# A row norm's small VectorE instructions moved to ScalarE, its guard to a 385th element of the row, and its overflow test to one place

## The chip, the core and the metric

The kernel runs on one core of a Trainium2 chip. A core has five engines with a queue of instructions each: TensorE (PE in the profile, PEld for its weight loads), VectorE (DVE), ScalarE (ACT), GpSimd (POOL) and SyncE (SP, which issues all DMAs here). Engines run side by side and wait for each other by semaphores; each works through its own queue in order. The metric is the device time of one execution in microseconds; lower is better.

## What is computed

A decaying linear attention over 4 sequences of 768 positions with 8 heads of 48, then two gated feed-forward layers on the 3072 rows of 384, the first behind a root-mean-square norm:

```python
for t in range(S):
    cur = np.einsum('bhd,bhe->bhde', u[None] * kt, vt)
    y[:, :, t] = np.einsum('bhd,bhde->bhe', rt, state + cur)
    state = w[None, :, :, None] * state + np.einsum('bhd,bhe->bhde', kt, vt)
...
rms = np.sqrt(np.mean(x * x, axis=-1, keepdims=True) + 1e-06)
xn = x / rms * rms_g
g = xn @ w_gate
x = (g / (1.0 + np.exp(-g)) * (xn @ w_val)) @ w_out
...
gate = 1.0 / (1.0 + np.exp(-(x @ w_gate2)))
out = (gate * (x @ w_val2)) @ w_out2
```

The weights are doubles (d_ff = 1536).

## The kernel before

**Tiles and stages.** The 3072 rows are 24 tiles of 128 (`attention(i)`, tile `i` is positions `128*(i // 4)` of sequence `i % 4`). Four tiles make a block of 512 rows; six blocks go through layer 1 and then six through layer 2. A step (`step`) is one block times one of the 12 slices of 128 of d_ff: 18 matmuls of 128x512 for gate and value (lines 687 to 689: high times high, high times low, low times high part of split fp32 operands) and 9 for the output (line 714). 144 steps stand behind each other on TensorE; the first needs all four tiles of block 0.

**One tile of attention.** `kq` and `rq` are k and r scaled by decay (line 474, on VectorE or GpSimd, whichever the planner finds free), turned by TensorE (line 332; ScalarE copies them out as `kT`, `rT`, line 498). Tiles 8 to 23 are turned by DMA through memory instead. `both` (lines 508 and 513) makes the products of 64 positions and the state's increments in two PSUM banks. VectorE masks the products (`aa`, line 519, one per bank), adds the state to the increments of the first bank (`zh`, line 529; for tiles 0 to 3, where there is no state yet, a plain copy, line 527) and then forms `zu` (line 532). `result` (lines 541, 548) makes the output, and VectorE adds the position's own term `vc` to it (line 554, two halves).

**The norm of a tile**, which is what the change is about: ScalarE squares the row and sums it (line 563; the sum is read out by a second, small instruction), VectorE tests the sum against 3e38 and keeps the verdict in `ok` (line 565), VectorE turns the sum into mean plus 1e-6 (line 568), GpSimd takes it to the power -0.5 (recorded under the helper's line 473), and VectorE scales the row (line 572). Then TensorE turns `x` (line 583) and ScalarE and VectorE write its high and low part `xh`, `xl` (lines 587, 589).

**The weights.** A piece is 128 rows of one of the three matrices as doubles. ScalarE (lines 66, 71), VectorE (lines 80, 81) and GpSimd (line 87) turn it into fp32, then ScalarE and VectorE split it (lines 649, 652). There are 36 pieces per layer; those of layer 1 are converted just ahead of the steps of block 0, those of layer 2 later.

**Order.** `Plan` collects tasks with an engine, a cost and a due time and runs them in a model of the engines; the order in which it starts them is the order of the instructions in the program, on every engine. So a task that costs less, goes to another engine or has other inputs can move all that stands behind it, SyncE's DMAs too. `V`, `A`, `G`, `T`, `S` are VectorE, ScalarE, GpSimd, TensorE and SyncE.

Of the kernel before, what the change touches and what calls it, by code (L numbers as in the profile page):

```python
# [7 lines left out]
F32 = mybir.dt.float32  # L8
# [3 lines left out]
AF = mybir.ActivationFunctionType  # L12
ALU = mybir.AluOpType
AX = mybir.AxisListType

P = 128
HS = 112
NPAIR = 4
EPS = 1e-6
# [211 lines left out]
def blocked(  # L231
# [17 lines left out]
    nc = tc.nc  # L249
    B, H, S, D = r.shape  # L250
    NT, DM = out.shape
# [11 lines left out]
    def ring(name, n, shape, dtype=F32):  # L263
        return [work.tile(shape, dtype, name=f"{name}{i}") for i in range(n)]
# [12 lines left out]
    ok = const.tile([P, 1], F32, name="ok")  # L277
    one = const.tile([P, 1], F32, name="one")
    totals = const.tile([P, 2 * 3 * NF], F32, name="totals")
    mhalf = const.tile([P, 1], F32, name="mhalf")  # L280

    rn, kn, vn = ring("rn", 2, [P, H, PAD]), ring("kn", 2, [P, H, PAD]), ring("vn", 3, [P, H, D])
    kq, rq, vc = ring("kq", 2, [P, H, PAD]), ring("rq", 1, [P, H, PAD]), ring("vc", 2, [P, H, D])
    cf, ss, small = ring("cf", 2, [P, H, 1]), ring("ss", 2, [P, 1]), ring("rms", 2, [P, 2])

    kT, rT, aa = ring("kT", 2, [HS, NPAIR, P]), ring("rT", 2, [P, NPAIR, P]), ring("aa", 1, [P, 2, NPAIR, P])
    x, z = ring("x", 2, [P, DM]), ring("z", B, [HS, NPAIR, D])

    zh, zu = ring("zh", 2, [HS, NPAIR, D]), ring("zu", 2, [HS, NPAIR, D])
    xh, xl = ring("xh", 2, [P, KC, N], F32R), ring("xl", 2, [P, KC, N], F32R)
# [26 lines left out]
    h = hi.bitcast(F32)  # L319

    def mul(e, out, x, y, op=ALU.mult):
        e.tensor_tensor(out=out, in0=x, in1=y, op=op)
# [11 lines left out]
    def setup():  # L334


        nc.vector.memset(o[0], 0.0)
        def warm(banks):
            for bank in banks:
                nc.tensor.matmul(state_of(plan.banks[bank]), o[0][:, :P], o[0][:, :NPAIR * D], start=True, stop=True)  # L340

        def turn_raw(bank, t):
            turn_pairs(plan.banks[bank], t)
            return pairs(plan.banks[bank])
        nc.vector.memset(wT, 1.0)
        for n in range(2):
            nc.sync.dma_start(out=wT[rows(n)], in_=w.rearrange("(p a) d -> a d p", a=2)[n])
        for t in (kn[0], rn[0], kq[1], rq[0]):
            nc.gpsimd.memset(t[:, :, D:], 0.0)
        load_heads(kn[0], k, 0, 0)  # L350
        load_heads(rn[0], r, 0, 0)
        nc.sync.dma_start(out=flat(u_bc), in_=u.rearrange("(o h) d -> o (h d)", o=1).to_broadcast([P, DM]))
        nc.sync.dma_start(out=g_bc, in_=rms_g.rearrange("(o c) -> o c", o=1).to_broadcast([P, DM]))
        nc.gpsimd.memset(mhalf, -0.5)
        nc.scalar.activation(one, mhalf, AF.Silu)
        nc.gpsimd.memset(ident, 0.0)
        nc.gpsimd.affine_select(out=ident, in_=ident, compare_op=ALU.not_equal, fill=1.0,
                                base=0, pattern=[[-1, P]], channel_multiplier=1)
# [12 lines left out]
        tp, tq = (t[:HS].rearrange("p (q t) -> p q t", q=NPAIR) for t in o[1:3])
        def lost(a, b):

            mul(nc.vector, sq[:, a:b], h[:, a - 1:b - 1], h[:, a - 1:b - 1])
            mul(nc.vector, low[:, a:b], sq[:, a:b], h[:, a:b], ALU.subtract)
            mul(nc.vector, twice[:, a:b], sq[:, a:b], h[:, a:b], ALU.add)

        def longer(e, s):
            n = 1 << s
            bc = p2[:, s].unsqueeze(2).to_broadcast([HS, NPAIR, n])  # L380
            if e is nc.vector:
                mul(e, tq[:, :, half - 2 * n:half - n], tq[:, :, half - n:half], bc)
# [12 lines left out]
        nc.vector.tensor_copy(p2[:, 0], wsafe)
        nc.vector.memset(tq[:, :, half - 1:half], 1.0)
        nc.gpsimd.memset(tp[:, :, half:half + 1], 1.0)
        mul(nc.vector, lo[:, 0], wsafe, h[:, 0], ALU.subtract)
        mul(nc.vector, both[:, 0], wsafe, h[:, 0], ALU.add)
        longer(nc.gpsimd, 0)  # L400
        lost(1, LOST)
        for i in range(1, 7):
            if i == LOST - 1:
                lost(LOST, 8)
            if i > 1:
                longer(nc.vector, i - 2)
            twofold(i)
            if i < 6:
                longer(nc.gpsimd, i)
        longer(nc.vector, 5)  # L410
        nc.vector.reciprocal(out=p2[:, 0], in_=p2[:, 6])
        bc = p2[:, 0].unsqueeze(2).to_broadcast([HS, NPAIR, half])
        mul(nc.vector, tq[:, :, half:], tq[:, :, :half], bc)
        mul(nc.gpsimd, tp[:, :, :half], tp[:, :, half:], bc)
        mul(nc.vector, kT[0], raw_k, tq)
        mul(nc.vector, rT[0][:HS], raw_r, tp)
        for i, (src, dst) in enumerate(((tq, wk), (tp, wr))):
            ps = plan.banks[i]
            for p in range(NPAIR):
                nc.tensor.transpose(ps[:, p * P:p * P + HS], src[:, p, :], ident[:HS, :HS])  # L420
            nc.scalar.activation(heads(dst), heads(ps.rearrange("p (h d) -> p h d", h=H)), AF.Copy)
# [43 lines left out]
    def attention(i):  # L465
# [58 lines left out]

        u3 = lambda sp: state_of(sp)[:HS].rearrange("p (q e) -> p q e", q=NPAIR)
        if first:
            add("V", 0.27, d + 4, lambda sp: nc.vector.tensor_copy(zh[i2], u3(sp)), [name("sp")], [("zh", i2)], psum=banks[:1])
        else:
            add("V", 0.27, d + 4, lambda sp: nc.vector.tensor_tensor(out=zh[i2], in0=u3(sp), in1=z[b], op=ALU.add),
                [name("sp"), ("z", b)], [("zh", i2)], psum=banks[:1])  # L530
# [27 lines left out]
        if not last:  # L558
            add("VG", (0.27, 0.6), d + 10, either(z[b], zu[i2], wc, ALU.mult), ["wc", ("zu", i2)], [("z", b)])


        t = ss[i2]
        add("A", 0.5, d + 7, lambda: nc.scalar.activation(flat(vc[i2]), x[i2], AF.Square, accum_out=t[:, 0:1]),
            [("x", i2)], [("vc", i2), ("ss", i2)])
        add("V", 0.07, d + 20, lambda: nc.vector.scalar_tensor_tensor(
            out=ok, in0=t[:, 0:1], scalar=3e38, in1=ok, op0=ALU.is_le, op1=ALU.mult), [("ss", i2)], ["ok"])
        t_ = small[i2]
        add("V", 0.07, d + 8, lambda: nc.vector.tensor_scalar(
            out=t_[:, 0:1], in0=t[:, 0:1], scalar1=1.0 / DM, scalar2=EPS, op0=ALU.mult, op1=ALU.add),
            [("ss", i2)], [("rms", i2)])  # L570
# [196 lines left out]
    def weights_ok():  # L767
        nc.vector.tensor_scalar(out=totals, in0=totals, scalar1=W_TOP * 2.0 ** -64, scalar2=None, op0=ALU.is_le)
        nc.vector.tensor_reduce(out=one, in_=totals, axis=AX.X, op=ALU.min)
        mul(nc.vector, ok, ok, one)  # L770
        nc.vector.tensor_scalar(out=ok, in0=ok, scalar1=-1.0, scalar2=1.0, op0=ALU.mult, op1=ALU.add)
        nc.vector.memset(one, 1.0)

# [7 lines left out]
    for n, (bi, f) in enumerate(steps):  # L781
# [9 lines left out]
                park_weights(*pieces[m], 3 * n + 6, begun)  # L791
            parks += PARK
        if (bi, f) == (turn - 1, NF - 1):
            plan.add("V", 0.6, at[turn, 3], weights_ok, [("total", i) for i in range(2 * 3 * NF)], ["ok"])
            plan.add("T", 0.1, at[turn, 3], count_bad, ["ok"], ["count"], psum=["count"])
            plan.add("V", 0.1, at[turn, 3], lambda ps: nc.vector.tensor_copy(bad, ps[:1, 0:1]), ["count"], psum=["count"])
        if bi == turn - 1:
# [168 lines left out]
```

## Time and profile before

| | |
|---|---|
| runs | 1031.54, 1032.00, 1032.87 us; median 1032.0 |
| profiled execution | 1029.34 us, its span 1027.7 us |
| busy: TensorE, its weight loads, VectorE, ScalarE, GpSimd | 98%, 81%, 48%, 33%, 14% of the span |
| mean granted clock of TensorE | 0.989 of full speed |
| chain that ended last | TensorE 87%, VectorE 8%, DMA 1%, ScalarE 1%, no wait shown 1% |

A busy share is the time in which at least one instruction of the engine was under way. Matmuls overlap and their ends are modelled, so TensorE is best read by its waits and by the starts of its instructions. The chain is followed back from the last instruction to whatever released each step.

### The profile page before, as it was taken

The page shows a single profiled execution, that of the slowest core. Times are in us where ns is not written, and L with a number is a line of the kernel's source. Part 1 is how long each engine was busy: PE and PEld are TensorE (multiplying, and loading weights), DVE is VectorE, ACT ScalarE, POOL GpSimd, SP SyncE. Part 2 cuts the span into 40 slices and gives each one's busy share as a digit, 9 for nine tenths or more (in the row PEclk, how much of TensorE's full clock was granted, in tenths as well). Part 3 has the DMA queues.
Part 4 walks back from the last instruction along what each step waited for, and adds up shares of the span by engine and source line. Part 5 has one row for each costly group of instructions (what it writes and reads, how often), then busy time and mean ns, then how long its engine had stood idle before and what let it go on. Part 6 is the DMA issues. An engine that isn't in the chain of part 4 may idle for free.

```text
span 1027.7 us, 19397 instructions
## 1 busy us (share of the span) xinstructions
PE 1002.4 (98%) x7938; PEld 831.1 (81%) x7938; DVE 490.4 (48%) x993; ACT 341.7 (33%) x710; POOL 140.2 (14%) x170
## 2 busy tenths in 40 slices
PE   7799999999999999999999999999999999999997
PEld 6577777787787777778888888888888888888886
DVE  7889995645655664653555322222222223222222
ACT  3577552223333333334555312222212222112221
POOL 4443432212321320211110000000000000000000
PEclk8899999999999999999999999999999999999998
DMA  8916356555884785653654100100100000000001
GB/s 195 274 41 157 91 110 143 106 104 129 178 175 123 156 189 135 145 148 94 198 171 147 62 1 3 59 1 22 40 1 31 32 1 5 27 1 27 4 1 34
DMA packets 213761, 91.40 MB, mean 89 GB/s; under 512 B 156576, under 2 KB 205984, under 8 KB 213664
## 3 DMA queue, kind: packets, MB, share of 16 engines
q1 hardware_dynamic: 213664, 90.08, 35.3%
q8 instruction: 64, 1.05, 0.5%
q14 instruction: 33, 0.27, 0.1%
HBM read 64.10 MB, written 25.95 MB: 88 GB/s over the span
## 4 chain that ended last, share of the span: by engine, by line
PE 87%; DVE 8%; DMA 1%; ACT 1%; issue 1%; POOL 0%; SPq 0%; DVEq 0%; POOLq 0%; ACTq 0%
PE bank L714 27%; PE bank L687 18%; PE bank L688 18%; PE bank L689 18%; PE bank L548 2%; DVE wraw L81 1%; PE bank L541 1%; PE bank L508 1%; DVE w L652 1%; DVE wt L80 1%; DVE hl L699 1%; DMA rn<-in_r_dram 1%; PE bank L513 1%; DVE vc L474 1%; DVE sg L696 0%
## 5 line engine op out<-in xcount | busy, mean ns | idle before, releaser
L687 PE MATMUL bank<-xh,w 128*128 128x512 f32 x864 | 344.5, 399 | 1.8 <-ACT w L649 1.1
L689 PE MATMUL bank<-xh,w 128*128 128x512 f32 x864 | 342.5, 396 | 0.3 <-DVE w L652 0.3
L688 PE MATMUL bank<-xl,w 128*128 128x512 f32 x864 | 342.6, 397 | 0.0
L696 DVE TENSOR_TENSOR sg<-bank,sg 128x512 f32<-128x512 f32 x144 | 99.2, 689 | 371.5 <-PE bank L689 368.2
L689 PEld LDWEIGHTS bank<-xh,w 128*128 128x128 f32 x864 | 162.7, 188 | 40.7 <-DVE w L652 2.3
L687 PEld LDWEIGHTS bank<-xh,w 128*128 128x128 f32 x864 | 162.8, 188 | 39.2 <-ACT w L649 2.4
L688 PEld LDWEIGHTS bank<-xl,w 128*128 128x128 f32 x864 | 162.8, 188 | 35.4 <-DVE xl L589 0.3
L694 ACT ACTIVATE sg<-bank 128x512 f32<-128x512 f32 x144 | 85.9, 597 | 294.0 <-PE bank L689 293.9
L698 ACT ACTIVATE hh<-sg 128x512 fp32r<-128x512 f32 x144 | 90.7, 630 | 238.5 <-DVE sg L696 238.5
L714 PE MATMUL bank<-w,hh 128*128 128x384 f32 x576 | 158.7, 337 | 0.0
L714 PE MATMUL bank<-hh,w 128*128 128x512 f32 x432 | 151.3, 401 | 0.7 <-DVE w L652 0.7
L699 DVE TENSOR_TENSOR hl<-sg,hh 128x512 fp32r<-128x512 f32 x144 | 102.2, 710 | 65.3 <-ACT hh L698 65.0
L714 PEld LDWEIGHTS bank<-w,hh 128*128 128x128 f32 x576 | 105.0, 188 | 3.4
L714 PEld LDWEIGHTS bank<-hh,w 128*128 128x128 f32 x432 | 81.0, 188 | 21.2 <-DVE w L652 1.6
L714 PE MATMUL bank<-w,hl 128*128 128x384 f32 x288 | 96.7, 336 | 0.0
L714 PE MATMUL bank<-hl,w 128*128 128x512 f32 x216 | 85.4, 395 | 0.0
L87 POOL TENSOR_TENSOR wt<-wraw 128x384 int32<-128x384 int32 x36 | 33.1, 918 | 200.1 <-DVE wraw L81 118.8
L66 ACT ACTIVATE wt<-wraw 128x384 f32<-128x384 f32 x72 | 39.7, 552 | 51.5 <-DMA wraw<-in_moe_w_gate_dram 23.0
L714 PEld LDWEIGHTS bank<-w,hl 128*128 128x128 f32 x288 | 54.1, 188 | 3.3 <-DVE hl L699 0.3
L714 PEld LDWEIGHTS bank<-hl,w 128*128 128x128 f32 x216 | 40.6, 188 | 8.7
L87 POOL TENSOR_TENSOR wraw<-wraw 128x384 int32<-128x384 int32 x36 | 37.8, 1060 | 54.4 <-DVE wraw L81 31.4
L81 DVE SCALAR_TENSOR_TENSOR wraw<-wraw,wt 128x384 int32<-128x384 int32 x72 | 41.8, 589 | 1.4
(122 smaller groups left out, 712.6 us busy)
## 6 DMA issues: line engine op xcount, KB each, us to landing
wraw<-in_moe_w_gate_dram SPq DMA_DIRECT2D x24, 384.0 KB, 4.4
wraw<-in_moe_w_val_dram SPq DMA_DIRECT2D x24, 384.0 KB, 4.5
wraw<-in_moe_w_out_dram SPq DMA_DIRECT2D x24, 384.0 KB, 5.0
parked<-wt SPq DMA_DIRECT2D x36, 192.0 KB, 2.7
wt<-parked SPq DMA_DIRECT2D x36, 192.0 KB, 2.4
kn<-in_k_dram SPq DMA_DIRECT2D x24, 192.0 KB, 3.7
rn<-in_r_dram SPq DMA_DIRECT2D x24, 192.0 KB, 4.1
vn<-in_v_dram SPq DMA_DIRECT2D x24, 192.0 KB, 3.8
```

The costliest lines, as they stand in the source:

```text
L66: nc.scalar.activation(t.bitcast(F32), raw[:, :, 1].bitcast(F32), AF.Abs, scale=2.0 ** -112, accum_out=total)
L81: yield nc.vector.scalar_tensor_tensor(out=high, in0=high, scalar=-(1 << 31), in1=t, op0=ALU.bitwise_and, op1=ALU.bitwise_or)
L87: nc.gpsimd.tensor_tensor(out=out, in0=raw[:, :, 1], in1=raw[:, :, 0], op=ALU.add)
L548: nc.tensor.matmul(yp[n][part(s)][ts, p * D:(p + 1) * D], aa[0][part(s), n, p, ts], vn[i3][part(s), 2 * p + n, :], start=(first and not s ...
L687: nc.tensor.matmul(ps, whi[f][:, kind, ws], xh[b2][:, c, :], start=(c == 0), stop=False)
L688: nc.tensor.matmul(ps, whi[f][:, kind, ws], xl[b2][:, c, :], start=False, stop=False)
L689: nc.tensor.matmul(ps, wlo[f][:, kind, ws], xh[b2][:, c, :], start=False, stop=(c == KC - 1))
L694: add("A", 0.6, d - STEP, lambda g: nc.scalar.activation(sg[n2], g, gate), [("g", n)], [("sg", n2)], psum=[("g", n)])
L696: add("V", 0.69, d + 1 - STEP, lambda ps: nc.vector.tensor_tensor(out=sg[n2], in0=ps, in1=sg[n2], op=ALU.mult), [("value", n)], [("sg", n2 ...
L698: add("A", 0.63, d + 1 - STEP, lambda: nc.scalar.activation(hh[n2], sg[n2], AF.Copy), [("sg", n2)], [("hh", n2)])
L699: add("VG", (0.69, 1.5), d + 1 - STEP, lambda e: by[e].tensor_tensor(out=hl[n2], in0=sg[n2], in1=hh[n2].bitcast(F32), op=ALU.subtract), [( ...
L714: nc.tensor.matmul(a[:, :rhs.shape[-1]], lhsT, rhs, start=(f == 0 and i == 0), stop=(f == NF - 1 and i == 2))
```

## The change

Three things. The copy of the state's increments for tiles 0 to 3 goes from VectorE to ScalarE. The tiles `x` and `vc` get a 385th column; that of `x` is set once by GpSimd, and ScalarE squares 385 elements of the row scaled by the root of 1/384, so that its sum is already the mean plus the guard; GpSimd's power reads that sum directly, and line 568 is gone. The sums of all 24 tiles are kept in `squares` and tested at once, with three VectorE instructions in `weights_ok`, in place of line 565 in every tile.

```diff
+    squares = const.tile([P, NTILE], F32, name="squares")
...
-    cf, ss, small = ring("cf", 2, [P, H, 1]), ring("ss", 2, [P, 1]), ring("rms", 2, [P, 2])
+    cf, small = ring("cf", 2, [P, H, 1]), ring("rms", 2, [P, 1])
...
-    x, z = ring("x", 2, [P, DM]), ring("z", B, [HS, NPAIR, D])
+    x_, vc_ = ring("x", 2, [P, DM + 1]), ring("vc", 2, [P, DM + 1])
+    x, vc = [t[:, :DM] for t in x_], [t[:, :DM].rearrange("p (h d) -> p h d", h=H) for t in vc_]
...
+        for t in x_:
+            nc.gpsimd.memset(t[:, DM:], (EPS * DM) ** 0.5)
...
         if first:
-            add("V", 0.27, d + 4, lambda sp: nc.vector.tensor_copy(zh[i2], u3(sp)), [name("sp")], [("zh", i2)], psum=banks[:1])
+            add("A", 0.27, d + 4, lambda sp: nc.scalar.activation(zh[i2], u3(sp), AF.Copy), [name("sp")], [("zh", i2)], psum=banks[:1])
...
-        t = ss[i2]
-        add("A", 0.5, d + 7, lambda: nc.scalar.activation(flat(vc[i2]), x[i2], AF.Square, accum_out=t[:, 0:1]),
-            [("x", i2)], [("vc", i2), ("ss", i2)])
-        add("V", 0.07, d + 20, lambda: nc.vector.scalar_tensor_tensor(
-            out=ok, in0=t[:, 0:1], scalar=3e38, in1=ok, op0=ALU.is_le, op1=ALU.mult), [("ss", i2)], ["ok"])
-        t_ = small[i2]
-        add("V", 0.07, d + 8, lambda: nc.vector.tensor_scalar(
-            out=t_[:, 0:1], in0=t[:, 0:1], scalar1=1.0 / DM, scalar2=EPS, op0=ALU.mult, op1=ALU.add),
-            [("ss", i2)], [("rms", i2)])
-        add("G", 0.55, d + 8, tt(nc.gpsimd, t_[:, 1:2], t_[:, 0:1], mhalf, ALU.pow), (), [("rms", i2)])
+        mean, t_ = squares[:, i:i + 1], small[i2]
+        add("A", 0.5, d + 7, lambda: nc.scalar.activation(vc_[i2], x_[i2], AF.Square, scale=DM ** -0.5, accum_out=mean),
+            [("x", i2)], [("vc", i2), ("square", i)])
+        add("G", 0.55, d + 8, tt(nc.gpsimd, t_, mean, mhalf, ALU.pow), [("square", i)], [("rms", i2)])
...
+        nc.vector.tensor_scalar(out=squares, in0=squares, scalar1=3e38 / DM, scalar2=None, op0=ALU.is_le)
+        nc.vector.tensor_reduce(out=one, in_=squares, axis=AX.X, op=ALU.min)
+        mul(nc.vector, ok, ok, one)
```

Line numbers of the changed kernel are a few higher: 474 becomes 480, 519 becomes 525, 554 becomes 560, 541 and 548 become 547 and 554.

**What moves.** VectorE, the last instructions ahead of the first step, whose matmuls need the fourth `xl` (tile 3; `x1` and `rms1` are tile 3's there, `x0` tile 2's, `bank3`, `bank1` with `aa0`, `zh0`, `zu0` are tile 4's, `w0` the first slice's weights). Before:

```order
L572 SCALAR_TENSOR_TENSOR x0_118<-x0_118,rms0_111,g_bc_85 128x384
L568 TENSOR_SCALAR rms1_112<-ss1_110 128x1
L565 SCALAR_TENSOR_TENSOR ok_91<-ss1_110,ok_91 128x1
L519 TENSOR_TENSOR aa0_117<-bank3_76,mask_87 128x4x64
L519 TENSOR_TENSOR aa0_117<-bank1_74,mask_87 128x4x64
L529 TENSOR_TENSOR zh0_124<-bank3_76,z0_120 112x192
L532 TENSOR_TENSOR zu0_126<-bank1_74,zh0_124 112x192
L589 TENSOR_TENSOR xl0_130<-bank6_79,xh0_128 128x3x128
L572 SCALAR_TENSOR_TENSOR x1_119<-x1_119,rms1_112,g_bc_85 128x384
L652 TENSOR_TENSOR w0_803<-wraw0_313,w0_803 128x384 x2
L589 TENSOR_TENSOR xl0_130<-bank2_75,xh0_128 128x3x128
```

Now:

```order
L80 TENSOR_SCALAR wt1_144<-wt1_144 128x384
L81 SCALAR_TENSOR_TENSOR wraw0_314<-wraw0_314,wt0_143 128x384
L589 TENSOR_TENSOR xl0_129<-bank2_75,xh0_127 128x3x128
L81 SCALAR_TENSOR_TENSOR wraw0_314<-wraw0_314,wt1_144 128x384
L572 SCALAR_TENSOR_TENSOR x1_116<-x1_116,rms1_109,g_bc_85 128x384
L80 TENSOR_SCALAR wt3_146<-wt3_146 128x384
L81 SCALAR_TENSOR_TENSOR wraw0_318<-wraw0_318,wt3_146 128x384
L589 TENSOR_TENSOR xl0_129<-bank3_76,xh0_127 128x3x128
L652 TENSOR_TENSOR w0_776<-wraw0_314,w0_776 128x384
```

Tile 4's masks and state stood ahead of the fourth `xl` and are now some 60 places behind it, among the steps; the split of the first weights moved behind it too. From the first mask of tile 1 on, 61 VectorE instructions stood up to and with the fourth `xl`; now there are 45.

TensorE at the same place (`vn1` with `aa0` and `z0` is tile 4's `result`, its `both` stands ahead of it; `x0` and `x1` are tiles 2 and 3). Before:

```order
L513 MATMUL bank1_74<-vn1_100,kq0_102 48x48
L583 MATMUL bank6_79<-ident_86,x0_118 128x128 x3
L541 MATMUL bank5_78<-z0_120,rT0_115 64x48
L548 MATMUL bank4_77<-vn1_100,aa0_117 32x48 x4
L583 MATMUL bank2_75<-ident_86,x1_119 128x128 x3
L687 MATMUL bank0_73<-xh0_128,w0_803 128x512
```

Now (`vn0` is tile 3's):

```order
L554 MATMUL bank7_80<-vn0_100,aa0_114 32x48 x4
L336 MATMUL bank6_79<-ident_86,kq0_103 112x128 x4
L583 MATMUL bank2_75<-ident_86,x0_115 128x128 x3
L583 MATMUL bank3_76<-ident_86,x1_116 128x128 x3
L687 MATMUL bank4_77<-xh0_127,w0_776 128x512
```

The first step stood behind all of tile 4's attention and now stands behind tile 3's; the turn of tile 4's `rq`, its `both` and its `result` come in steps 3 to 5.

VectorE at tile 1, with the engine whose semaphore each waits for. Before:

```order
L519 TENSOR_TENSOR aa0_117<-bank6_79,mask_87 128x4x64 [waits PE_49]
L519 TENSOR_TENSOR aa0_117<-bank7_80,mask_87 128x4x64 [waits PE_49]
L527 COPY zh1_125<-bank6_79 112x192
L568 TENSOR_SCALAR rms0_111<-ss0_109 128x1 [waits Activation_49]
L474 TENSOR_TENSOR vc1_106<-vn1_100,cf1_108 128x384 [waits DMAHW1_49]
```

Now:

```order
L525 TENSOR_TENSOR aa0_114<-bank6_79,mask_87 128x4x64 [waits Activation_49]
L480 TENSOR_TENSOR rq0_105<-rn0_96,wr_89 128x8x48 [waits DMAHW7_49]
L480 TENSOR_TENSOR vc1_118<-vn1_101,cf1_107 128x384 [waits DMAHW1_49,DVE_49]
L525 TENSOR_TENSOR aa0_114<-bank7_80,mask_87 128x4x64 [waits PE_49]
```

The first mask of each of tiles 0 to 3 waits for ScalarE's copy out of the same bank, and VectorE no longer stands at line 568 for ScalarE's sum.

## Rows read from the trace of the kernel before

**Rows 1.** Stretches of the span: us, busy us (instructions) of each engine, clock, DMA share.

```profile
core 0: us, PE busy (x) PEld busy (x) DVE busy (x) ACT busy (x) POOL busy (x), PEclk, DMA share, GB/s
0.00:46.10 46.10, 33.01 (x820) 27.94 (x820) 36.70 (x129) 19.27 (x51) 19.47 (x39) 0.85 0.93 223
46.10:150.00 103.90, 99.38 (x867) 76.22 (x868) 99.22 (x196) 68.82 (x170) 44.30 (x44) 0.98 0.44 110
150.00:360.00 210.00, 209.99 (x2529) 167.25 (x2528) 125.23 (x274) 62.10 (x132) 46.23 (x52) 1.00 0.65 139
...
470.00:1028.00 558.00, 550.15 (x2580) 472.03 (x2578) 166.79 (x265) 153.66 (x273) 9.87 (x11) 0.99 0.13 42
```

**Rows 2.** TensorE's timeline around the first step: start, us, line, [idle <- releaser].

```profile
41.38 0.26 PE L541 MATMUL bank<-zh,rT 48*64 48x48 f32 x2 [0.84 <-DVE zh L529]
...
46.11 0.79 PE L687 MATMUL bank<-xh,w 128*128 128x512 f32 x1 [0.58 <-ACT xh L587]
```

**Rows 3.** What TensorE waited for in 46:160: us in total, times, longest.

```profile
PE bank L687 <- ACT w L649: 1.1, 2, 0.8
PE bank L508 <- DVE xl L589: 0.8, 1, 0.8
...
PE bank L583 <- DVE x L572: 0.6, 1, 0.6
```

**Rows 4.** Two stretches of VectorE's load, columns as in rows 1.

```profile
20.55:46.09 25.54, 17.48 (x564) 14.09 (x564) 22.28 (x61) 11.24 (x29) 11.36 (x13) 0.87 1.00 262
46.11:138.30 92.19, 88.27 (x819) 67.51 (x819) 87.55 (x177) 63.76 (x160) 39.53 (x40) 0.98 0.44 113
```

**Rows 5.** VectorE's groups in 20.5:46: xcount | busy us, mean ns | idle before.

```profile
L519 DVE TENSOR_TENSOR aa<-bank,mask 128x256 f32<-128x256 f32 x8 | 3.1, 413 | 0.0
L565 DVE SCALAR_TENSOR_TENSOR ok<-ss,ok 128x1 f32<-128x1 f32 x4 | 1.7, 424 | 0.0
L527 DVE COPY zh<-bank 112x192 f32<-112x192 f32 x3 | 1.0, 347 | 0.0
L652 DVE TENSOR_TENSOR w<-wraw,w 128x384 fp32r<-128x384 f32 x2 | 1.0, 551 | 0.0
L568 DVE TENSOR_SCALAR rms<-ss 128x1 f32<-128x1 f32 x4 | 0.6, 146 | 0.0
```

**Rows 6.** The chain that ended last, in order of time: start, us, what.

```profile
14.01 6.85 DMA rn<-in_r_dram
...
148.21 2.10 PE bank L714 x9
```

**Rows 7.** TensorE's groups in 150:250.

```profile
L687 PE MATMUL bank<-xh,w 128*128 128x512 f32 x81 | 32.6, 403 | 0.0
L714 PE MATMUL bank<-hh,w 128*128 128x512 f32 x79 | 27.7, 402 | 0.0
L714 PE MATMUL bank<-hl,w 128*128 128x512 f32 x40 | 15.8, 395 | 0.0
L508 PE MATMUL bank<-rT,kT 48*64 48x64 f32 x192 | 4.2, 224 | 0.0
```

**Rows 8.** VectorE's groups in 46.6:140.

```profile
L565 DVE SCALAR_TENSOR_TENSOR ok<-ss,ok 128x1 f32<-128x1 f32 x4 | 2.3, 563 | 0.0
L474 DVE TENSOR_TENSOR vc<-vn,cf 128x384 f32<-128x384 f32 x3 | 2.3, 756 | 0.0
L474 DVE TENSOR_TENSOR kq<-kn,wk 128x384 f32<-128x384 f32 x4 | 2.2, 546 | 0.0
L568 DVE TENSOR_SCALAR rms<-ss 128x1 f32<-128x1 f32 x4 | 0.6, 144 | 0.0
```

**Rows 9.** ScalarE's groups over the whole span, shapes apart.

```profile
L498 ACT ACTIVATE rT<-bank 112x512 f32<-112x512 f32 x7 | 4.2, 595 | 4.8 <-PE bank L332 4.8
L421 ACT ACTIVATE wk<-bank 128x384 f32<-128x384 f32 x1 | 0.5, 491 | 4.6 <-PE bank L420 4.6
```

More of the change, by code (lines that the diff above doesn't have):

```diff
@@ L279, in blocked @@
     totals = const.tile([P, 2 * 3 * NF], F32, name="totals")
+    squares = const.tile([P, NTILE], F32, name="squares")
     mhalf = const.tile([P, 1], F32, name="mhalf")
     rn, kn, vn = ring("rn", 2, [P, H, PAD]), ring("kn", 2, [P, H, PAD]), ring("vn", 3, [P, H, D])
-    kq, rq, vc = ring("kq", 2, [P, H, PAD]), ring("rq", 1, [P, H, PAD]), ring("vc", 2, [P, H, D])
-    cf, ss, small = ring("cf", 2, [P, H, 1]), ring("ss", 2, [P, 1]), ring("rms", 2, [P, 2])
+    kq, rq = ring("kq", 2, [P, H, PAD]), ring("rq", 1, [P, H, PAD])
+    cf, small = ring("cf", 2, [P, H, 1]), ring("rms", 2, [P, 1])
     kT, rT, aa = ring("kT", 2, [HS, NPAIR, P]), ring("rT", 2, [P, NPAIR, P]), ring("aa", 1, [P, 2, NPAIR, P])
-    x, z = ring("x", 2, [P, DM]), ring("z", B, [HS, NPAIR, D])
+    x_, vc_ = ring("x", 2, [P, DM + 1]), ring("vc", 2, [P, DM + 1])
+    x, vc = [t[:, :DM] for t in x_], [t[:, :DM].rearrange("p (h d) -> p h d", h=H) for t in vc_]
+    z = ring("z", B, [HS, NPAIR, D])
     zh, zu = ring("zh", 2, [HS, NPAIR, D]), ring("zu", 2, [HS, NPAIR, D])
@@ L559, in attention @@
             add("VG", (0.27, 0.6), d + 10, either(z[b], zu[i2], wc, ALU.mult), ["wc", ("zu", i2)], [("z", b)])
-        t = ss[i2]
-        add("A", 0.5, d + 7, lambda: nc.scalar.activation(flat(vc[i2]), x[i2], AF.Square, accum_out=t[:, 0:1]),
-            [("x", i2)], [("vc", i2), ("ss", i2)])
-        add("V", 0.07, d + 20, lambda: nc.vector.scalar_tensor_tensor(
-            out=ok, in0=t[:, 0:1], scalar=3e38, in1=ok, op0=ALU.is_le, op1=ALU.mult), [("ss", i2)], ["ok"])
-        t_ = small[i2]
-        add("V", 0.07, d + 8, lambda: nc.vector.tensor_scalar(
-            out=t_[:, 0:1], in0=t[:, 0:1], scalar1=1.0 / DM, scalar2=EPS, op0=ALU.mult, op1=ALU.add),
-            [("ss", i2)], [("rms", i2)])
-        add("G", 0.55, d + 8, tt(nc.gpsimd, t_[:, 1:2], t_[:, 0:1], mhalf, ALU.pow), (), [("rms", i2)])
+        mean, t_ = squares[:, i:i + 1], small[i2]
+        add("A", 0.5, d + 7, lambda: nc.scalar.activation(vc_[i2], x_[i2], AF.Square, scale=DM ** -0.5, accum_out=mean),
+            [("x", i2)], [("vc", i2), ("square", i)])
+        add("G", 0.55, d + 8, tt(nc.gpsimd, t_, mean, mhalf, ALU.pow), [("square", i)], [("rms", i2)])
         add("V", 0.53, d + 9, lambda: nc.vector.scalar_tensor_tensor(
-            out=x[i2], in0=x[i2], scalar=t_[:, 1:2], in1=g_bc, op0=ALU.mult, op1=ALU.mult), [("rms", i2)], [("x", i2)], port=True)
+            out=x[i2], in0=x[i2], scalar=t_, in1=g_bc, op0=ALU.mult, op1=ALU.mult), [("rms", i2)], [("x", i2)], port=True)
         to = (slice(None), slice(None), slice(col * P, (col + 1) * P))
@@ L793, in blocked @@
         if (bi, f) == (turn - 1, NF - 1):
-            plan.add("V", 0.6, at[turn, 3], weights_ok, [("total", i) for i in range(2 * 3 * NF)], ["ok"])
+            plan.add("V", 0.6, at[turn, 3], weights_ok, [("total", i) for i in range(2 * 3 * NF)] + [("square", i) for i in range(NTILE)], ["ok"])
             plan.add("T", 0.1, at[turn, 3], count_bad, ["ok"], ["count"], psum=["count"])
```

## The prediction

> **What bounds the kernel now.** I read the busy shares first, then the load by stretches, since a share of 98% for TensorE says nothing of where the other 2% are. From 150 us on TensorE is busy without a gap, up to a single short wait and the kernel's tail, while VectorE has 40% of its time free and later 70% [rows 1]. Nothing that the change takes from VectorE there can move the end. Ahead of 150 us it is otherwise: up to 46 us TensorE is idle for 13 of 46 us, and from 46 to 150 VectorE is busy for 95% and TensorE loses 4.5 us [rows 1]. So the kernel has three parts: a start that ends with the first step, at 46.11 us [rows 2]; a stretch in which VectorE (weights, attention and the steps' own work) nearly sets the pace; and a long rest that belongs to TensorE. The time is, in effect, the start of the first step, plus all of TensorE's work behind it, plus what it waits in the second part.
>
> Both early parts show this norm. The last links ahead of the first step are ScalarE's `xh` and, before that, a `result` that waited for VectorE's `zh` [rows 2]; that `result` is tile 4's, which block 0 does not need, but it stands ahead of the first step in TensorE's queue. In the second part TensorE waits for split weights, for `xl`, and once for a row scaled by line 572 [rows 3].
>
> **The change, part by part.**
>
> *What the instructions cost.* Line 568 takes 0.15 us. Line 565 takes as little when VectorE is alone, but its mean is 0.42 us in the start and 0.56 us in the second part [rows 5, 8], where GpSimd works beside it. Up to 140 us the trace has eight of each: 1.7 + 2.3 us for line 565, 0.6 + 0.6 us for line 568. Four copies `zh` of 0.35 us are 1.4 us more [rows 5], where three of the four are. Together VectorE loses 6.6 us of work ahead of 140 us. That is the most that the bare removal could give if VectorE were the whole path there, and nothing is the least. The sixteen norms behind 140 us have TensorE's unbroken work as their cover; if that went, 16 x 0.3 us would be at stake. The three instructions of the common test run once, some 550 us in, under the same cover.
>
> *What is added.* ScalarE's four copies are bounded by what they replace, 0.35 us, and by a copy of 128x384 out of PSUM, 0.49 us [rows 9]; I take 0.4, near the lower, since the tile is half as wide. ScalarE is busy for 11 of the 25 us around them [rows 4], so its time is free. The 385th element and the two settings by GpSimd I cost at nothing: GpSimd is idle for over half of the start [rows 1]. The copy brings a wait, though: the mask of the same bank now waits for ScalarE, and all of VectorE's queue behind it. One copy (0.4) and two masks (0.33 each from start to start, by their mean of 0.41 less the overlap) are 1.06 us from `both` to the last of the three, against 0.33 + 0.33 + 0.35 = 1.01 us before: even. The trace of before has no bank that two engines read without a dependency of their own, so no row shows whether such a wait is needed. The Trainium skill's page "PSUM — Partial Sum Buffer" (PSUM bank collisions raise a hardware error) says that two engines must not touch one bank at the same time and that software has to keep them apart; by that rule the wait stays, and an overlap that would save some 0.3 us on each of four tiles is not to be had.
>
> *What moves: the start.* This is the largest term. The planner now puts tile 4's masks, `zh`, `zu`, `both` and `result` behind the first step. From 20.55 us to the fourth `xl` VectorE took 25.54 us, of which 22.28 were busy, in 61 instructions [rows 4]. In the new order 17 of them are no longer there. I subtract them at their means [rows 5]: line 565 1.7, line 568 0.6, three copies 1.0, three masks 1.2 (two of tile 4; the first of tile 1 comes ahead of my starting point), tile 4's `zh` and `zu` 0.7 (as the copy, 0.35 each), two splits of weights 1.0, one shift of weights 0.45; and add two products and one merge of weights that come in, at 0.55 each for a product of 128x384 [rows 8], and 0.4 more since the exchange of products with GpSimd is uneven. 22.3 - 6.65 + 2.05 = 17.7 us; the `rq` that now begins the list waits for its r, which landed at 20.86 us [rows 6]. Without any idle time the fourth `xl` would so come at 38.6 us, with the 3.3 us of idle time of before at 41.9. The other engines allow it: TensorE was busy for 17.5 of the 25.5 us with tile 4's work in them, ScalarE and GpSimd for 11 [rows 4]. I take 40.2, the middle, and the first step with it: 46.1 - 40.2 = 5.9 us earlier, between 7.5 and 4.2.
>
> *What moves: TensorE's work.* Tile 4 has not gone, it is behind the first step now. In 150:250 TensorE ran 3 x 81 matmuls of lines 687 to 689 (688 and 689 have as many as 687) and 119 of line 714, and six tiles of attention (192 records of line 508, 32 for each) [rows 7]. At 2.10 us for nine [rows 6], 0.233 us each, the 362 take 84.5 us, which leaves 15.5 us, or 2.6 for a tile. With the turn of `rq`, half a microsecond, 3.1 us go back.
>
> *What moves: VectorE's stretch.* Up to the last x of block 1, at 138.3 us, VectorE is busy for 87.6 of 92.2 us and TensorE idle for 3.9 [rows 4]. There VectorE loses 2.3 + 0.6 us [rows 8]. It gains tile 4's two masks (0.8), `zh` and `zu` (0.7), one split (0.55) and, counted in the new order, four more products (0.55 to 0.76 each [rows 8], 2.6): 4.7 us. Net 1.8 us more, while TensorE's own work there grows by 3.1. Where VectorE sets the pace, TensorE's idle time would shrink by 1.3 us; where single late weights do, it stays. I take 0.4 us of gain. What is late next is the same as now: splits of weights (line 652) for steps 1 to 3, with VectorE one split behind where it stood at the first step.
>
> *DMAs.* The loads of tile 6's k and r now stand ahead of the weights of slice 7 in SyncE's queue and wait until VectorE has used tile 4's; the first split of slice 7 stands 31 places behind that use in VectorE's queue, some 15 us at half a microsecond each, and a load of this size took 6.85 us to land when the queues were full [rows 6], so I cost it at nothing; without that slack it would be about those 7 us, which the range covers in part.
>
> *Sum.* 5.9 - 3.1 + 0.4 = 3.2 us off. The profiled execution took 1029.34 us, so it would take 1026.1; the median of the runs is 2.7 us above it, and 1032.0 - 3.2 gives **1028.8 us**.
>
> **The rivals.**
>
> *The start gains only what it displaces (no change).* If VectorE meets more collisions with GpSimd, as the scaled row does, or the weights' splits hold the first step at 43 us, the 3.1 us of tile 4 eat it all: 1032.0, within 1.5. For it: the middle of a range of 3.3 us is a choice. Against it: 17 instructions fewer are a fact of the order.
>
> *VectorE is overdrawn in its stretch (slower).* The place is steps 1 to 11. VectorE was already at 95%; tile 4's 4.7 us come fully onto the path as TensorE's waits for `xl` and weights, and the lighter norm was not on it. With the first step at the late end, 41.9: 4.2 - 3.1 - 4.7 = -3.6, or 1035.6 us. It decides from the point where TensorE's idle time there grows from 3.9 to over 7.
>
> *VectorE lets go altogether (much faster).* If taking out the instructions that stand and wait (565 for GpSimd, 568 for ScalarE) frees VectorE for good, TensorE's idle time of 3.9 us goes too: 7.5 - 3.1 + 3.9 = 8.3, or 1023.7 us. For it: GpSimd now starts its power as soon as ScalarE is done. Against it: the first waits are for weights, which the change does not touch.
>
> *The change does not do what it says:* the removed instructions were only where VectorE waited in any case, and the planner's order is as good as before: 1032.0; part of the first rival.
>
> **How the numbers follow.** About 0.2% (2.1 us) is what a measurement of this kernel can tell from no change. My forecast, 2 to 6 us off, has 0.48; no change (within 2 us) 0.24; the overdrawn stretch 0.19; the large gain 0.09. The forecast's low edge lies at the bound, so faster by over 0.2% is 0.57, within it 0.25, slower 0.18. The range that leaves out some 2 in 10 runs from 1024.0, just above the large gain, to 1034.5, into the slower case.
>
> **What would show it.** In the new profile: the first matmul of line 687 at 39 to 42 us instead of 46.11; nothing of lines 568 and 565; ScalarE's copies near 0.4 us, with masks waiting for them; tile 4's `result` behind the matmuls of slice 5; VectorE's share between the first step and 140 us still over 93%, and TensorE's idle time there near 3.5 us; no gap behind 150 us. I am wrong in the start if the first step comes at 43 us or later, and in the stretch if TensorE's waits there exceed 6 us or fall below 1.5.

## The result and the profile after

The changed kernel takes **1015.19 us** (median of four runs, 1012.69 to 1018.28) against 1031.77 for the kernel before beside it: a ratio of 0.9845, 95% interval 0.9824 to 0.9866. It is 16.6 us faster, where 3.2 were forecast, and below the predicted range. Its profiled execution was the slowest of the four, 1018.28 us with a span of 1016.5; that of before was its fastest, 1029.34 with 1027.7. So the two traces show 11.2 us of the 16.6.

Line numbers have moved by 4 to 6 in places: 508 is now 514, 519 is 525, 527 is 533, 541 is 547, 548 is 554, 474 is 480. The load by stretches, columns as in [rows 1]:

```profile
core 0: us, PE busy (x) PEld busy (x) DVE busy (x) ACT busy (x) POOL busy (x), PEclk, DMA share, GB/s
0.00:46.80 46.80, 33.05 (x656) 28.01 (x656) 31.82 (x111) 19.47 (x54) 19.93 (x40) 0.72 0.91 220
46.80:150.00 103.20, 97.86 (x1019) 76.83 (x1020) 97.23 (x198) 67.96 (x169) 42.49 (x43) 0.98 0.41 110
150.00:360.00 210.00, 210.00 (x2548) 170.57 (x2547) 125.76 (x255) 64.58 (x136) 45.64 (x50) 1.00 0.64 141
470.00:1016.00 546.00, 538.98 (x2561) 469.16 (x2559) 167.01 (x265) 151.71 (x268) 9.03 (x10) 1.00 0.13 43
```

VectorE lost 4.9 us of work in the start, as the change says. But the start is no shorter: TensorE's timeline, as in [rows 2], has the first step at 46.82 us instead of 46.11.

```profile
32.75 0.45 PE L554 MATMUL bank<-vn,aa 64*32 64x48 f32 x21 [2.39 <-issue]
...
38.95 1.02 PE L554 MATMUL bank<-vn,aa 64*32 64x48 f32 x40 [2.15 <-issue]
...
44.90 0.90 PE L583 MATMUL bank<-ident,x 128*128 128x128 f32 x3 [3.25 <-DVE x L572]
46.82 0.79 PE L687 MATMUL bank<-xh,w 128*128 128x512 f32 x1 [1.02 <-ACT w L649]
```

Behind it, in 46.8:160, TensorE waits longer than in [rows 3]:

```profile
PE bank L687 <- ACT w L649: 3.1, 3, 1.3
PE bank L689 <- DVE w L652: 1.2, 2, 0.8
PE bank L547 <- DVE zh L535: 1.2, 2, 1.0
```

So up to the thirteenth step (the first of block 1) the changed kernel is 3.0 us **behind**: its first L687 comes at 144.78 us, against 141.75. From there to the last step it gains 14.1 us, in stretches where TensorE hardly idled before either, and step by step: 0.18 us in each step of layer 1 and 0.05 in each of layer 2. What changed is how often a matmul comes. In the chain that ended last (start, us, what), steps without attention work repeat like this, in the kernel before:

```profile
481.31 2.10 PE bank L714 x9
487.62 2.10 PE bank L714 x9
...
701.73 2.09 PE bank L714 x12
708.01 2.09 PE bank L714 x12
```

and in the changed one:

```profile
482.71 2.04 PE bank L714 x9
488.83 2.04 PE bank L714 x9
...
699.43 2.10 PE bank L714 x12
705.66 2.10 PE bank L714 x12
```

A layer-1 step went from 6.30 to 6.12 us. It has 27 matmuls of 128x512: **233.3 ns each before, 226.7 now**. I call the time from one matmul's start to the next one's the pitch. A layer-2 step went from 6.28 to 6.23. The clock is 1.00 of full speed on both sides in 150:360, the shapes and the count of matmuls are the same. The question for the experiments was what else a norm's rewriting can do to a matmul.

### The profile page after: what moved, and what is told of

The parts are those of the page before. It is cut to its first block, busy times and chain, and to the rows that moved or that the text cites. A ratio compares the mean times of both kernels' runs of the same rounds, so it can differ in the third digit from the quotient of the medians.

```text
span 1016.5 us, 19338 instructions
## 1 busy us (share of the span) xinstructions
PE 989.9 (97%) x7938; PEld 834.2 (82%) x7938; DVE 484.0 (48%) x950; ACT 342.4 (34%) x714; POOL 138.2 (14%) x166
## 4 chain that ended last, share of the span: by engine, by line
PE 89%; DVE 4%; issue 2%; DMA 2%; ACT 1%; POOL 1%; SPq 0%; DVEq 0%; POOLq 0%
PE bank L714 28%; PE bank L687 19%; PE bank L689 18%; PE bank L688 18%; PE bank L554 2%; PE bank L514 1%; PE bank L547 1%; DMA wraw<-in_moe_w_val_dram 1%; DVE w L652 1%; PE bank L519 1%; DVE wraw L81 1%; DVE wt L80 0%; ACT wt L66 0%; ACT wraw L71 0%; DMA rn<-in_r_dram 0%
## 5 line engine op out<-in xcount | busy, mean ns | idle before, releaser
L687 PE MATMUL bank<-xh,w 128*128 128x512 f32 x864 | 340.3, 394 | 3.4 <-ACT w L649 3.1
L689 PE MATMUL bank<-xh,w 128*128 128x512 f32 x864 | 339.2, 393 | 1.3 <-DVE w L652 1.2
L688 PE MATMUL bank<-xl,w 128*128 128x512 f32 x864 | 338.3, 392 | 0.0
L687 PEld LDWEIGHTS bank<-xh,w 128*128 128x128 f32 x864 | 162.7, 188 | 37.3 <-ACT w L649 4.3
L688 PEld LDWEIGHTS bank<-xl,w 128*128 128x128 f32 x864 | 162.7, 188 | 32.0
L714 PE MATMUL bank<-w,hh 128*128 128x384 f32 x576 | 159.2, 337 | 0.0
L714 PE MATMUL bank<-hh,w 128*128 128x512 f32 x432 | 149.3, 396 | 0.0
L714 PEld LDWEIGHTS bank<-w,hh 128*128 128x128 f32 x576 | 105.3, 188 | 2.8
L714 PE MATMUL bank<-w,hl 128*128 128x384 f32 x288 | 96.8, 336 | 0.0
L714 PEld LDWEIGHTS bank<-hh,w 128*128 128x128 f32 x432 | 81.1, 188 | 17.5
L714 PE MATMUL bank<-hl,w 128*128 128x512 f32 x216 | 84.1, 389 | 0.0
L714 PEld LDWEIGHTS bank<-w,hl 128*128 128x128 f32 x288 | 54.1, 188 | 3.0 <-DVE hl L699 0.3
L714 PEld LDWEIGHTS bank<-hl,w 128*128 128x128 f32 x216 | 40.6, 188 | 7.7
```

What stands on the lines that cost most here:

```text
L687: nc.tensor.matmul(ps, whi[f][:, kind, ws], xh[b2][:, c, :], start=(c == 0), stop=False)
L688: nc.tensor.matmul(ps, whi[f][:, kind, ws], xl[b2][:, c, :], start=False, stop=False)
L689: nc.tensor.matmul(ps, wlo[f][:, kind, ws], xh[b2][:, c, :], start=False, stop=(c == KC - 1))
L714: nc.tensor.matmul(a[:, :rhs.shape[-1]], lhsT, rhs, start=(f == 0 and i == 0), stop=(f == NF - 1 and i == 2))
```

## The experiments

Two things about the matmuls changed: which instructions run beside them, and where their operands lie. The new tile `squares` takes 96 bytes in each partition, ahead of the weights; behind the weights `ss` is gone (2 x 32 bytes) and four rows of `x` and `vc` take 1,568 bytes instead of 1,536. So the weights moved by 96 bytes, and the activations `xh`, `xl`, `hh`, `hl` by 96 - 64 + 128 = 160. In the built programs `xh0` begins 108,224 bytes behind `w0` before and 108,288 after. Modulo 512 that is 192 and 256, the same for every weight tile, column block and activation tile, as their sizes are all multiples of 512. I call it the distance.

All times in one table. "Step 1" and "step 13" are the first L687 of these steps, "rest" is from step 13 to step 144, all three from the profiled execution; nine L714 from the chain near 480 us. "Changed" and "before" name the order of instructions. Each ratio is to the kernel before as it ran in the same round, with medians there of 1031.77 (changed), 1030.79 (e1 to e4), 1030.74 (e5 to e7, a1), 1032.04 (e8, c1, c2, b3) and 1031.37 us (f1, f2). In e3 and e4 the lines lie one further down, so that L687 is L688 there and L714 is L715.

| kernel | distance | median us | ratio to before [95%] | step 1 | step 13 | rest | nine L714 |
|---|---|---|---|---|---|---|---|
| before | 192 | 1031.77 | 1 | 46.11 | 141.75 | 869.62 | 2.10 |
| changed | 256 | 1015.19 | 0.9845 [0.9824, 0.9866] | 46.82 | 144.78 | 855.47 | 2.04 |
| before, all + 96 (e1) | 192 | 1030.31 | 0.9988 [0.9973, 1.0004] | 46.76 | 143.48 | 868.91 | 2.10 |
| changed, all + 32 (e2) | 256 | 1017.23 | 0.9872 [0.9849, 0.9895] | 43.56 | 142.09 | 856.34 | 2.04 |
| before (e3) | 224 | 1030.47 | 1.0001 [0.9990, 1.0013] | 46.42 | 142.56 | 869.48 | 2.10 |
| before (e4) | 288 | 1031.64 | 1.0006 [0.9993, 1.0019] | 45.92 | 141.50 | 870.13 | 2.10 |
| before (e5) | 256 | 1020.38 | 0.9888 [0.9857, 0.9920] | 47.81 | 145.25 | 858.12 | 2.04 |
| changed (e6) | 192 | 1030.15 | 0.9994 [0.9982, 1.0006] | 43.39 | 145.51 | 869.86 | 2.10 |
| before (e7) | 0 | 1019.08 | 0.9897 [0.9873, 0.9921] | 45.95 | 142.11 | 857.80 | 2.04 |
| before (e8) | 384 | 1031.95 | 1.0000 [0.9983, 1.0017] | 45.68 | 142.25 | 870.34 | 2.10 |
| changed, `zh` on VectorE (a1) | 256 | 1018.74 | 0.9895 [0.9862, 0.9928] | 40.64 | 142.17 | 857.29 | 2.04 |
| changed again (c1) | 256 | 1015.28 | 0.9843 [0.9821, 0.9866] | 43.61 | 141.31 | 856.50 | 2.04 |
| before (c2, as e5) | 256 | 1018.18 | 0.9865 [0.9846, 0.9884] | 45.23 | 142.61 | 858.23 | 2.04 |
| changed, 4 raw buffers (b3) | 256 | 1018.58 | 0.9864 [0.9845, 0.9884] | 41.99 | 142.01 | 859.30 | 2.04 |
| before, `xh`, `xl` alone (f1) | 256 / 192 | 1020.67 | 0.9895 [0.9866, 0.9924] | 45.14 | 141.57 | 859.83 | 2.10 |
| before, `hh`, `hl` alone (f2) | 192 / 256 | 1029.66 | 0.9992 [0.9977, 1.0007] | 46.28 | 142.22 | 867.98 | 2.06 |

### A first theory that fell: a tile's own address

```diff
-    totals = const.tile([P, 2 * 3 * NF], F32, name="totals")
+    totals = const.tile([P, 2 * 3 * NF + 24], F32, name="totals")[:, :2 * 3 * NF]
```

That is e1; e2 widens `squares` in the changed kernel by 8 columns in the same way. No instruction moves.

> The kernel before, same instructions in the same order; one constant tile (totals) is 24 columns wider, so that every tile behind it lies 96 bytes further on: weights and activations begin at a multiple of 64 bytes instead of 32 behind one. Address theory (the changed kernel's faster matmuls come from where their operands lie): matmul pitch falls from 233 to 227 ns, 1011 to 1016 us. Order theory (they come from which instructions run beside them): pitch stays 233 ns, 1030 to 1033 us. Chip-or-clock theory (the runs of the changed kernel met a better moment): 1030 to 1033 us here, and a changed kernel that is slower again beside it.

> The changed kernel, same instructions in the same order; its new constant tile is 8 columns wider, so that everything behind it lies 32 bytes further on, weights and activations again 32 bytes behind a multiple of 64, as in the kernel before. Address theory: pitch returns to 233 ns and the time to what the change costs by itself, 1031 to 1036 us (the first 141 us of the changed kernel took 3.0 us longer). Order theory: stays at 1013 to 1018 us.

Both went against the address theory: 1030.31 and 1017.23 us, the pitch with the program and not with the address. e3 and e4 moved one of the two operands against the other, by 32 and by 96 bytes (with an unused `ring("gap", ...)` ahead of `xh`).

> The kernel before; only the weight tiles (and all that lies ahead of the activations) move by 96 bytes to a multiple of 64; 32 bytes more ahead of the activations put those back to where they were by 128. If the weight loads (stationary operand) make the pitch: 1013 to 1018 us. If the moving operand makes it: 1030 to 1033 us in layer 1's share, and at most the layer-2 output matmuls, which stream weights, gain (4 us). If both must lie well: no gain.

> The kernel before; only the activations (xh, xl, sg, hh, hl) move by 96 bytes to a multiple of 64, the weights stay. If the moving operand makes the pitch: 1013 to 1018 us (the layer-2 output matmuls alone, which stream weights, stay). If the weight loads make it: 1030 to 1033 us. If both add: halfway, some 1023 us.

Neither gained: 1030.47 and 1031.64 us. But between e1, e2 and the two programs the distance had not changed, and in e3 and e4 it was 224 and 288, neither the old one nor the new one. So the four runs still left a distance theory beside the order theory.

### The distance

```diff
-    xh, xl = ring("xh", 2, [P, KC, N], F32R), ring("xl", 2, [P, KC, N], F32R)
+    ring("gap", 1, [P, 16]); xh, xl = ring("xh", 2, [P, KC, N], F32R), ring("xl", 2, [P, KC, N], F32R)
```

This is e5, 64 unused bytes in the kernel before. e6 puts 112 columns there in the changed kernel, e7 80 and e8 48 in the kernel before; every engine's instructions stand as they stood.

> The kernel before, same instructions in the same order; an unused tile of 64 bytes ahead of the activations moves xh, xl, sg, hh, hl by 64 bytes against the weights. From the start of a weight tile to the start of an activation it is then 256 bytes modulo 512, as in the changed kernel; it was 192 before (and in the kernel with everything moved by 96), 224 and 288 where only weights or only activations moved by 96 or so. Distance theory (the pitch of the matmuls is set by the distance of the two operands in the partition, since each matmul streams one while the next one's weights are loaded): pitch 227 ns, time 1011 to 1016 us. Order theory (something that the change moved sets it): 233 ns, 1029 to 1033 us.

> The changed kernel, same instructions in the same order; an unused tile of 448 bytes ahead of the activations gives the distance of the kernel before, 192 bytes modulo 512. Distance theory: pitch 233 ns, time 1031 to 1036 us, the change's own price without the matmuls' gain. Order theory: stays at 1013 to 1018 us.

> The kernel before with the distance at 0 modulo 512. Distance theory with a period of 256 bytes or less: pitch 227 ns, 1011 to 1016 us; with 256 as the only good distance of 512: 233 ns or slower, 1030 us and more. Order theory: no change, 1029 to 1033 us.

> The kernel before with the distance of the operands at 384 bytes modulo 512, that is 128 modulo 256. If the period is 128 bytes: pitch 227 ns, 1016 to 1021 us. If it is 256: pitch 233 ns, 1029 to 1033 us.

The distance theory held four times in the pitch. Of the times, e6 came 1 us below the range that I gave it, and e5 and e7 came 3 to 4 us above theirs: I had given the kernel before the changed kernel's whole time. 64 unused bytes make the kernel before 10 us faster, and the changed kernel with the old distance is no faster than the kernel before: 1030.15 us, ratio 0.9982 to 1.0006. The chain of e6 has the old pitch again:

```profile
485.31 2.10 PE bank L714 x9
491.62 2.10 PE bank L714 x9
```

0 and 256 are fast; 192, 224, 288 and 384 are slow. That is a period of 256 bytes, as far as six distances tell.

### Which operands

The gaps had moved every later tile too. f1 leaves `xh` and `xl` at 256 and puts the rest back with a second gap ahead of `sg`; f2 has only the 64 bytes ahead of `sg`.

```diff
-    sg, hh, hl = ring("sg", 2, [P, N]), ring("hh", 2, [P, N], F32R), ring("hl", 2, [P, N], F32R)
+    ring("gap2", 1, [P, 112]); sg, hh, hl = ring("sg", 2, [P, N]), ring("hh", 2, [P, N], F32R), ring("hl", 2, [P, N], F32R)
```

> The kernel before; a 64-byte gap puts xh and xl at the distance of 256 bytes from the weights, a second gap of 448 bytes behind them puts sg, hh, hl and all later tiles back to where they were modulo 512. Pair theory (each matmul's pitch follows from its own two operands): the matmuls of lines 687 to 689, which read xh and xl beside a weight, come every 227 ns, those of line 714 in layer 1, which read hh and hl, stay at 233; 18 of a layer-1 step's 27 matmuls gain, so two thirds of the layer-1 gain and most of layer 2's: 1020 to 1024 us. Whole-program theory (some one tile or the whole layout sets a state that all matmuls share): all at 227 ns and 1016 to 1020 us, or all at 233 and 1029 to 1033 us.

> The kernel before; the 64-byte gap stands behind xh and xl, so that only sg, hh, hl and later tiles come to the distance of 256 bytes, xh and xl stay at 192. Pair theory: lines 687 to 689 stay at 233 ns, line 714 in layer 1 comes every 227; a third of the layer-1 gain: 1025 to 1030 us. Whole-program theory: all at 227 ns and 1016 to 1020 us, or all at 233 and 1029 to 1033 us.

The pair theory held. TensorE's timeline (start, us, line) has, in f1, nine matmuls of line 714 from 490.63 to 492.74 and the next eighteen of the hidden layer up to 496.83, that is 234 and 227 ns each:

```profile
490.63 0.39 PE L714 MATMUL bank<-hh,w 128*128 128x512 f32 x1
...
492.74 0.39 PE L687 MATMUL bank<-xh,w 128*128 128x512 f32 x1
...
496.83 0.39 PE L714 MATMUL bank<-hh,w 128*128 128x512 f32 x1
```

and in f2 the other way round, 229 and 233 ns:

```profile
492.65 0.39 PE L714 MATMUL bank<-hh,w 128*128 128x512 f32 x1
...
494.71 0.39 PE L687 MATMUL bank<-xh,w 128*128 128x512 f32 x1
...
498.91 0.39 PE L714 MATMUL bank<-hh,w 128*128 128x512 f32 x1
```

Each matmul's pitch follows from its own two operands, but for a start-up: in both runs the first five matmuls behind the slower kind still come unevenly, which is why f2 has 229 and not 227. Its nine pitches are 226, 236, 228, 233 and 231 ns, and then four of 226 or 227. Of f2's gain only 1.7 us is to be seen in the medians, within the noise; its rest is 1.6 us shorter than that of before. In the trace, the load of the next weights (`PEld`) runs beside a matmul; the timeline of the changed kernel has a pair that begins together:

```profile
494.56 0.39 PE L689 MATMUL bank<-xh,w 128*128 128x512 f32 x1
494.56 0.19 PEld L714 LDWEIGHTS bank<-hh,w 128*128 128x128 f32 x1
```

So one operand streams while the other kind is loaded. That the two reads get in each other's way would explain why their distance counts, but no run shows the inside of it, nor why the period is 256; that stays open.

### What the change is worth by itself

> The changed kernel as it is, for a direct comparison with the kernel before at the same distance of operands (next run) on one chip. Own-gain theory (the change is worth some 2 to 4 us by itself once the matmuls are at their faster pitch): 1015 to 1017 us, 2 to 4 us under the next run. Nothing-by-itself theory (as at the slow pitch, where changed kernel and kernel before agreed within 0.2%): both within 1.5 us of each other, 1016 to 1020 us.

> The kernel before with 64 bytes ahead of the activations, distance 256 as in the changed kernel. Own-gain theory: 1018 to 1021 us, 2 to 4 us over the changed kernel. Nothing-by-itself theory: 1016 to 1020 us, within 1.5 us of it.

At the same good distance the changed kernel took 1015.28 and the kernel before 1018.18 us. The medians are 2.9 us apart, as the own-gain theory has it, but the two intervals overlap. All runs at a good distance together say more: the 13 executions of the changed order (the four of the result, e2, c1) have a mean of 1016.2 us, the 13 of the order before (e5, e7, c2) one of 1018.9. That is 2.6 us, with a 95% interval of 1.1 to 4.1, though not all of them ran in the same round. At the slow distance (e6) the change is worth nothing that can be measured. By the table, c1 is 1.6 us ahead of c2 at step 1 and 1.3 at step 13, and 1.7 us shorter in the rest. The rest is where the two orders differ throughout: 855.47 to 856.50 us in the three traces of the changed order, 857.80 to 858.23 in the three of the order before. TensorE's waits behind 145 us are part of it: 0 to 0.8 us against 0.7 to 1.3. What makes up the other part is open.

> The changed kernel with the copy of the first chunks' state (line 533) back on VectorE, everything else as changed; the tiles lie where they lie in the changed kernel. Distance theory: pitch stays 227 ns. The copy's own share: in the changed kernel VectorE waited 2.9 us for ScalarE's copies in the start; if that moved the first step, it comes up to 2 us earlier, 1012 to 1015 us; if the start is set by something else, 1014 to 1017 us. Order theory, with this copy as the cause of the faster pitch: 233 ns, 1028 us and more.

With the copy of `zh` back on VectorE the first step came at 40.64 us. That is 2.8 to 3.0 us earlier than in c1, e2 and e6 (43.4 to 43.6), but only 1.4 earlier than in b3 below (41.99), whose order on VectorE is the changed kernel's up to there. Nor is the copy all that differs: the planner also gave a1 another order (118 VectorE instructions ahead of the first step, not 111), and its mean granted clock in 20.55:40 was 0.97 of full speed, against 0.88 in b3, 0.80 in e6, 0.74 in c1 and 0.68 in e2 and the changed kernel. So the copy's price is not isolated. The earlier step bought nothing: step 13 came at 142.17, and the median is 1018.74, above the 1012 to 1017 of both theories of the start. My guess for what stands in between was the weights of block 0. In a1 and in e6 TensorE waits for those of the twelfth step; the timeline of e6:

```profile
137.14 0.50 PE L687 MATMUL bank<-xh,w 128*128 128x512 f32 x1 [2.97 <-ACT w L649]
```

and its chain just ahead of that, where the load of those weights starts once VectorE has freed a raw buffer:

```profile
129.38 0.06 DVE w L652
...
129.91 6.09 DMA wraw<-in_moe_w_val_dram
```

```diff
-RAWS, WTS = 3, 4
+RAWS, WTS = 4, 4
```

> The changed kernel with four instead of three buffers for raw weights. The stretch up to the thirteenth step (first L687 there at 142.1 to 144.8 us in every kernel so far, whether the first step came at 40.6 or at 46.8) ends with waits for the weights of the twelfth step, of 2.9 us where the first step came early. Weights theory (an earlier start buys nothing because the weights of the first block come at their own pace): with a fourth buffer the loads are asked for earlier, the wait goes, the thirteenth step comes 2 to 4 us earlier and the time is 1012 to 1014 us. VectorE theory (the stretch is set by VectorE's conversions, which no buffer makes faster): the wait moves to another step, 1015 to 1018 us.

The weights theory fell: a fourth buffer took the long wait away, step 13 stayed at 142.01, and TensorE waited elsewhere in 41.9:142. The median is 1018.58, just above the 1015 to 1018 of the VectorE theory. VectorE was busy for 94.3 of the 100 us from 42 on.

```profile
PE bank L687 <- ACT w L649: 1.8, 2, 1.0
PE bank L714 <- ACT hh L698: 1.5, 1, 1.5
PE bank L689 <- DVE w L652: 1.3, 2, 0.8
```

This fits VectorE as what sets the pace of that stretch. It was not tested by taking work from VectorE there alone. No version beat the changed kernel.

## Why the prediction was wrong

**The step that failed is the third part of the first paragraph:** the time is the first step's start "plus all of TensorE's work behind it", with that work taken as the same in both kernels. The rest does belong to TensorE: in 150:360 it is busy all the time after the change too. And "nothing that the change takes from VectorE there can move the end" is not what failed. What failed is the constant: 0.233 us for each matmul [rows 6]. The change moved it to 0.227 in layer 1 by resizing tiles, which has nothing to do with the norm's arithmetic. No term of the sum and no rival had that. In the runs it is worth 10 to 14 us (e5, e7 and c2 against the kernel before beside them: 10.4, 11.7 and 13.9), of 16.6.

**The sum of the change's own terms** was 3.2 us. At the new distance the medians are 2.9 us apart, at the old one 0.6, with an interval of about 2 us faster to 0.6 slower. Over all runs at a good distance they are 2.6 us apart (1.1 to 4.1). So the forecast's size fits at one distance and is not shown at the other, and that it fits is in part luck, since its path was not the one that I described:

- *The start, 5.9 us.* VectorE had 45 instructions up to the first step, as counted ahead of the prediction, and 18.85 us of work, where I had 17.7. (The prediction's "17" instructions fewer is a slip: its list takes 19 out and brings 3 in, 16 fewer.)

```profile
20.55:46.80 26.25, 17.09 (x424) 13.46 (x416) 18.85 (x45) 11.15 (x31) 10.77 (x12) 0.63 0.97 253
...
L560 DVE TENSOR_TENSOR x<-bank,vc 128x192 f32<-128x192 f32 x6 | 2.1, 353 | 4.0 <-PE bank L554 4.0
```

  What I mis-sized is its idle time: 7.4 us, where my bounds had 0 to 3.3. The step came at 41.99 to 43.61 in four executions with the changed kernel's order up to there (b3, e6, e2, c1), against 40.2 forecast, and at 46.82 in the profiled one. There TensorE also stood for 4.5 us ("issue") in tile 2's and 3's `result`, and its mean granted clock was 0.63 of full speed against 0.87 in [rows 4]. Of VectorE's 7.4 us of idle time 4.0 are waits for a `result`. So the term that I had at 0 to 3.3 us is not a constant of the program but differs from one execution to the next.
- *ScalarE's copy, "even".* It takes 0.33 us (0.4 forecast). But the masks waited for it, and VectorE's queue behind them: by the copy's own view,

```profile
L533 ACT ACTIVATE zh<-bank x4: 331/332/332, 15.0 to 34.4; 112x192 f32<-112x192 f32 x4
...
who waited for it (us, times):
  DVE aa L525: 2.9, 2
```

  That wait was missing in my sum: I had priced one copy and two masks from start to start as if ScalarE always began at once. It came to 1.2 to 3.5 us in the five traces with that copy (b3, c1, e2, the changed kernel, e6). The Trainium skill ("PSUM — Partial Sum Buffer", PSUM bank collisions raise a hardware error) has the rule behind it: no two engines may be at one bank at the same time, and semaphores have to keep them apart. The trace agrees so far as the masks stood behind a copy that reads their bank; no run kept ScalarE's copy without the wait. What it cost the first step is not shown: in a1, where the copy is VectorE's, that step came 1.4 to 6.2 us earlier than in these five, at another order and a higher granted clock.
- *Tile 4 given back, 3.1, and the stretch.* The rival "the start gains only what it displaces" is what held in the stretch: step 13 came at 141.3 to 145.5 us in all programs, whether step 1 came at 40.64 or at 47.81. VectorE's share up to 141.3 us is 93.7% (88.54 of 94.48 us), above the 93% that I named; TensorE waited 6.2 us in all in 46.8:160, above the 6 from which I called myself wrong there (5.9 in c1). The slower case, with VectorE overdrawn, did not come: at the old distance (e6) the change costs nothing in the end.
- *What was costed at nothing* stayed there: the common test, the 385th element, and, at the old distance, the removed work behind 150 us (from step 13 to step 144 e6 took 869.86 us, the kernel before 869.62).

## What to carry to other kernels

When a change resizes, adds or drops a tile, every later tile moves. Before you credit the instructions, put the old layout under the new program and the new layout under the old one; a few unused bytes do it. Where a kernel is bound by back-to-back matmuls, work out the distance between stationary and moving operand, try a few values, and read the pitch from the trace: here 64 bytes were worth more than the whole rewriting. And an earlier start is worth only what the next stretch can take from it.

## What was not expected of the hardware

- The pitch of 128x512 fp32r matmuls depends on the distance of their two operands in the partition: in layer 1, 226.7 ns at 0 and 256 bytes modulo 512, 233.3 at 192, 224, 288 and 384, with the same instructions in the same order. In layer 2 those of the hidden layer come every 229.1 ns at 256 (changed kernel), where the first nine of a step's eighteen, behind those of line 714 with another shape, come unevenly.
- In layer 2, where line 714 streams weights of 384 columns and loads `hh`, the same distance does not help: twelve take 2.10 us at 256 (changed) and 2.08 in f1, where `hh` is at 192 and `xh` at 256. A step of f1 there takes 6.20 us, of the changed kernel 6.23, of the kernel before 6.28:

```profile
701.88 2.08 PE bank L714 x12
708.08 2.08 PE bank L714 x12
```
- TensorE's gaps that the profile puts down to "issue" look like waits for instructions. In the sixteen traces 27 gaps of over 0.3 us up to 60 us have no releaser. All end at places that lie a whole multiple of 256 weight loads and matmuls apart in TensorE's stream, each 1.2 to 1.9 us after a packet of the queue that the page calls "instruction" has landed. In the changed kernel packets landed at 31.30 and 37.46 us, and the two gaps of line 554 ended at 32.75 and 38.95. The page has 64 such packets of 16 KB on that queue, for TensorE's 15,876 loads and matmuls:

```profile
q8 instruction: 64, 1.05, 0.5%
```

  So the 4.5 us of "issue" in the profiled execution are not shown to be a price of the norm. That the full DMA queues (share 0.97) held these packets up was not tested by a run.
